# Attention and a mixture of experts in one kernel: the exponentials' transposes directly behind the scores, the other turns last

## The chip, the cores and the metric

The kernel runs on one core of one Trainium2 chip. A core has five engines with an instruction stream each: TensorE (PE, matrix products; its weight loads are listed as PEld), VectorE (DVE), ScalarE (ACT), GpSimd (POOL) and SyncE (SP, which only issues DMAs). Data lies in HBM, in SBUF, and, for results of TensorE, in PSUM banks. The metric is the device time of one execution in microseconds; times are given as the median of several runs.

## The reference

Attention over q, k, v of 4 x 8 heads, 576 rows and 64 columns, with a memory part, feeds a mixture of experts; the casts and the setup are left out:

```python
scores = scale * np.matmul(q, k.transpose(0, 1, 3, 2))
scores = np.where(causal, -1000000000.0, scores)
a = np.exp(scores - scores.max(-1, keepdims=True))
a /= a.sum(-1, keepdims=True) + 1e-09
local = np.matmul(a, v)
q_p = phi(q)                       # x + 1 for x > 0, else exp(x)
mem_ret = np.einsum('bhsd,bhde->bhse', q_p, M_prev)
mem_norm = np.einsum('bhsd,bhd->bhs', q_p, z_prev)[..., None] + 1e-06
x = g * (mem_ret / mem_norm) + (1 - g) * local     # g = sigmoid(beta), by head
...
noisy_logits = x @ w_gate + np.log1p(np.exp(x @ w_noise)) * noise
top2 = np.argpartition(-noisy_logits, 2, axis=1)[:, :2]
for e in range(8):
    for k in range(2):
        mask = top2[:, k] == e
        h = np.maximum(x[mask] @ w1[e], 0.0)
        out[mask] += top2_w[mask, k, None] * (h @ w2[e])
```

The x that goes into the experts has 2304 rows of 512 columns; each expert's hidden layer has 1024.

## The kernel before

Products are made in float32 out of three products of split operands: a high part (names ending in `h`), and the rest (`l`). So scores are `kT` times `qh`, `ql`, `qh` (L540; L531 for the short row blocks), and an expert's products are named `ha`, `hb` (first layer, L928) and `y` (second layer, L941).

**Attention.** A batch has 576 rows, five row blocks: four of 128 rows and a short one of 64. A row block's eight heads are cut into units: two units of four heads for the first two blocks, four units of two heads for the others. A unit's path is: scores on TensorE; row maxima with the mask on VectorE (L546); exponentials on ScalarE (L569, one instruction and a read of the row's sum per head); `trans`, which turns the exponentials by transposes on TensorE into a bank `tpa` (L587), four 128 x 128 blocks to a bank, and empties it on ScalarE into `aT` (L588); and the product with V into `avT` (L609).

The loop runs over units, as a pipeline: in one round, unit u + 1 has its exponentials, unit u its transposes, u - 2 its product with V, and u + 2 its scores. Beside this pipeline, each row block has work of its own that is done in the rounds. `q_turn` and `k_turn` transpose q and k (`tpq`, `tpk`, L420) and ScalarE reads them out (`qf`, L452, and `kf`, L427); of `kf` come the high and low halves `kT` (L432, L433; for the short block on ScalarE and VectorE, for the others on GpSimd). `tpm` (L477) is the memory part, read out by ScalarE as `mm` (L480). When all units of a block are done, ScalarE copies the output (`xo`, L618), `out_turn` transposes it (`tpo`, L642) and VectorE reads it out with the sums' reciprocals (`xr`, L644, L646). Then the block's logits follow in steps, held in a queue `xq`: x is transposed (`tpx`, L136), read out in two halves `xTlh` (ScalarE, L139) and `xTll` (VectorE, L140), multiplied with the gate's weights (`tpl`, L147 and L148), read out (`lt`, L150), transposed back (`tpL`, L155) and read out (`ll`, L157). At the end of a batch the routing starts: small VectorE steps, and products (`pp`, L227) of a mask `M` with a triangle to count slots. They stand in a queue `small`, from which a round takes two while a flag `fast` is set (for the third batch's routing). `puts` writes slots' row numbers into tables in HBM with GpSimd DMAs; gathers by GpSimd (L816) bring the rows of an expert, which `xprep` transposes (`tpm` of L865).

All turns (`tpa`, `tpo`, `tpq`, `tpk`, `tpm`, `tpx`, `tpl`, `tpL`, `pp`) share one pool of three PSUM banks. TensorE's order is that in which the code is written, since its instructions are chained; the other engines' orders are set by the scheduler. The weights of the first expert (`w0q` and `w0k`) are loaded and split (`w2ha`, `w2hb`, L892) during the last row blocks.

What else a round does beside scores and product with V was put into a list `xs`, in this order:

```python
xs = due                                    # out_turn of a finished block
# ... xprep, sums, fills, ev (q_turn, k_turn, memory, ...) by their due times
for _ in range(1 if c < len(chunks) - 2 else 2):
    if xq: xs.append(xq.popleft())          # a logit step
xs += trans(u)
if len(xq) > 3 and c < len(chunks) - 2:
    xs.append(xq.popleft())
```

**Experts.** Each expert has 608 slots in five tiles, three of 128 and two of 112. They run in passes (an expert and some of its tiles; the first four passes are (0; 0, 1, 2), (1; 0, 1, 2), (1; 3, 4), (0; 3, 4)), each in eight slots f, one per 128 of the hidden width. A tile's rows are turned in time for its pass: at its `begin` slot VectorE casts them and SP issues two DMA transposes (`trn`, L1028), at its `ready` slot ScalarE copies them (`xf`, L1039) and makes `xTh` (L1042), and VectorE makes `xTl` (L1043). A table names the slots (p, f) of both for passes 1 to 4.

Of the kernel before, what the change touches and what calls it, by code (L numbers as in the profile page):

```python
# [46 lines left out]
def tile_attention_moe(ctx: ExitStack, tc: tile.TileContext, q, k, v, M_prev, z_prev, beta,  # L47
# [78 lines left out]
    puts = deque()  # L126
    R = {"XT0": []}
# [190 lines left out]
    def attention():  # L318
        with ExitStack() as c2:
# [31 lines left out]
            chunks = [(b, i) for b in range(B) for i in range(NCH)]  # L351
# [344 lines left out]
            fills, small, xq, held = deque(), deque(), deque(), deque()  # L696
# [34 lines left out]
            def smalls():  # L731

                for _ in range(2 if R.get("fast") else 1):
                    if small:
                        in_turn(small.popleft())

# [7 lines left out]
            for u in range(NU + 2):  # L744
                if u + 1 < NU:
                    expo(u + 1)
                ys, end = [], []
                due = [held.popleft()] if held else []
                if u >= 2:
                    ys += av(u - 2)  # L750
                    cl = units[u - 2][0]
                    if u > NU or units[u - 1][0] != cl:
                        ys.append(lambda cl=cl: out_copy(cl))
                        (held if cl < len(chunks) - 3 else end).append(lambda cl=cl: out_turn(cl))
                if u + 2 < NU:
                    ys += score(u + 2)
                n_ = next((k_ for k_, f in enumerate(ys) if f.__name__ == "products"), len(ys) - 1) + 1
                ys = [lambda fs=ys[:n_]: [f() for f in fs]] + ys[n_:] + end
                xs = due
                if u >= NU - 2 and u <= NU:  # L760
                    xs.append(lambda t=u - NU + 2: xprep(R["XT0"], R["xgE"][t], t))
                if u < NU:
                    c, hs = units[u]
                    if u == first[c]:
                        on_chunk(c)
                    if chunks[c] == (B - 1, 4) and u == first[c]:
                        for f in range(2):
                            W0.append(load_w(None, 0, f, None, None, [
                                ap_.tile([P, H, D], F32, tag=nm + "n", name="w0" + nm, bufs=4) for nm in "kq"]))
                    if chunks[c] == (B - 1, 4) and u == first[c] + 1:  # L770
                        W0[:] = [split_w(ep, W0[0], "a", 1), split_w(ep, W0[1], "b", 1)]
                    if chunks[c][1] == 4 and (u + 1 == NU or units[u + 1][0] != c):
                        xs.append(lambda c=c: sums(c))
                    la = 4 if u < 3 else 7
                    nxt = units[u + la][0] if u + la < NU else -1
                    while any(f[0] <= nxt for f in fills):
                        xs.append(fills.popleft()[1])
                    while ev and ev[0][0] < TU[u + 1]:
                        xs.append(ev.popleft()[2])
                    for _ in range(1 if c < len(chunks) - 2 else 2):  # L780
                        if xq:
                            xs.append(xq.popleft())
                    if puts:
                        xs.append(lambda: puts and puts.popleft()())
                    xs += trans(u)
                    if len(xq) > 3 and c < len(chunks) - 2:
                        xs.append(xq.popleft())
                    if puts and R.get("fast"):
                        xs.append(lambda: puts and puts.popleft()())
                nx, ny = len(xs), max(1, len(ys))  # L790
                done = 0
                for y, f in enumerate(ys):
                    in_turn(f)
                    smalls()
                    while done * ny < (y + 1) * nx:
                        in_turn(xs[done])
                        done += 1
                        smalls()
                for f in xs[done:]:
                    in_turn(f)  # L800
# [95 lines left out]
    def experts(tail):  # L896
        with ExitStack() as c3:
# [152 lines left out]
                    gather_y(g, tall[:, e, t, 1:2], e * CAP)  # L1050

            begin, ready = {}, {}
            for p, l in ((1, ((0, (0, 1), (0, 4)), (1, (0, 2), (0, 5)), (2, (0, 3), (0, 6)))),
# [4 lines left out]
                for t, s_, e_ in l:  # L1058
                    begin.setdefault(s_, []).append((p, t))
                    ready.setdefault(e_, []).append((p, t))  # L1060
# [107 lines left out]
            with tc.For_i(0, over, 1):  # L1168
# [6 lines left out]
                with tc.For_i(1, nround, 1) as r:  # L1175
                    with tc.For_i(0, E, 1) as e:
# [26 lines left out]
                        for t in every:  # L1203
# [9 lines left out]
                                in_offset=None, bounds_check=NTOK - 1, oob_is_err=False)  # L1213

    tail = attention()
    experts(tail)


# [26 lines left out]
```

## Time and profile before

| | before |
|---|---|
| median of 3 runs | 743.59 us (743.22 to 746.72) |
| profiled execution: its time | 748.14 us |
| its span | 746.4 us |
| mean granted clock of TensorE | 0.974 |
| TensorE busy | 696.5 us (93%), 5046 instructions |
| weight loads busy | 598.2 us (80%) |
| VectorE busy | 453.1 us (61%) |
| ScalarE busy | 378.7 us (51%) |
| GpSimd busy | 366.8 us (49%) |

The span runs from the first instruction's start to the last one's end in the profiled execution; 1.7 us of its time lie outside. Attention fills the span to about 287 us, the experts the rest. The granted clock is the share of TensorE's full speed that the chip let it run at. A busy share is a mean over both parts and says little of either.

### The profile page before, as it was taken

What the parts mean: (1) busy time and instruction counts of PE and PEld (TensorE: products, weight loads), DVE (VectorE), ACT (ScalarE), POOL (GpSimd) and SP (SyncE); (2) the same over time, 40 slices, a digit from 0 to 9 for tenths busy, and PEclk for the clock granted to TensorE, in tenths of its full rate; (3) what the DMA queues carried; (4) which work ended last, traced back from release to release, by engine and by line L of the source; (5) the groups of instructions that cost most, each with busy time, mean ns of one, the idle gap of its engine ahead of it and who ended that gap; (6) DMA issues with size and microseconds to landing.
All of it is one profiled execution on the core that took longest, in us unless ns stands there. A gap on an engine that the chain in (4) does not pass through costs nothing. (4 is left out here: it accounts for less than half of the span.)

```text
span 746.4 us, 14446 instructions
## 1 busy us (share of the span) xinstructions
PE 696.5 (93%) x5046; PEld 598.2 (80%) x5046; DVE 453.1 (61%) x1232; ACT 378.7 (51%) x949; POOL 366.8 (49%) x378
## 2 busy tenths in 40 slices
PE   5999989998889789989999999999999999999993
PEld 4778767876777578879788888898889889988992
DVE  5675777568677667967694687454455355454312
ACT  4797778787768653445554144153253163162210
POOL 6424434641843544565354686843833734625502
PEclk8899999999989999999999999999999999999997
DMA  7634521251300045869995595693694694665201
GB/s 167 140 93 107 123 64 42 62 126 45 72 30 28 11 138 148 190 140 264 180 247 151 140 234 150 177 210 115 182 197 135 163 218 148 190 128 172 71 0 63
DMA packets 174287, 98.19 MB, mean 132 GB/s; under 512 B 113172, under 2 KB 152596, under 8 KB 174208
## 3 DMA queue, kind: packets, MB, share of 16 engines
q1 hardware_dynamic: 164128, 78.23, 42.6%
q0 software_dynamic: 10080, 18.98, 10.3%
q8 instruction: 42, 0.69, 0.4%
q14 instruction: 37, 0.30, 0.1%
HBM read 74.41 MB, written 22.54 MB: 130 GB/s over the span
## 5 line engine op out<-in xcount | busy, mean ns | idle before, releaser
L891 POOL TENSOR_TENSOR w1lm<-w1sm,w1hm 128x512 fp32r<-128x512 f32 x72 | 93.4, 1301 | 115.2 <-DVE w1hm L890 62.4
L941 PE MATMUL y<-w2hm,hTh 128*128 128x512 f32 (+1 forms) x310 | 122.2, 394 | 1.2 <-ACT hTh L931 1.2
L941 PE MATMUL y<-w2hm,hTl 128*128 128x512 f32 (+1 forms) x310 | 122.3, 394 | 0.4 <-DVE hTl L932 0.4
L941 PE MATMUL y<-w2lm,hTh 128*128 128x512 f32 (+1 forms) x310 | 121.5, 392 | 0.0
L546 DVE CUSTOM_DVE_ANT_0 sc<-sc,mask 128x128 f32<-128x128 f32 (+4 forms) x144 | 75.3, 524 | 48.9 <-PE sc L531 21.1
L931 ACT ACTIVATE hTh<-ha 128x304 fp32r<-128x304 f32 (+2 forms) x64 | 27.2, 426 | 147.0 <-PE ha L928 146.9
L892 ACT CAST w2hm<-w2sm 128x512 fp32r<-128x512 f32 x74 | 45.8, 619 | 97.8 <-PE y L941 97.8
L893 DVE TENSOR_TENSOR w2lm<-w2sm,w2hm 128x512 fp32r<-128x512 f32 x74 | 61.5, 831 | 52.0 <-ACT w2hm L892 52.0
L569 ACT ACTIVATE a<-sc,nb 128x128 f32<-128x128 f32 (+4 forms) x144 | 79.1, 566 | 11.2 <-DVE nb L546 5.8
L890 DVE CAST w1hm<-w1sm 128x512 fp32r<-128x512 f32 x74 | 37.0, 499 | 62.5 <-PE hb L928 45.7
L587 PE MATMUL tpa<-identr,a 128*128 128x128 f32 x400 | 61.3, 287 | 13.8 <-DVE xr L644 4.7
L928 PE MATMUL ha<-xTl,w1hm 128*128 128x304 f32 (+2 forms) x224 | 68.9, 307 | 2.0 <-DVE xTl L1043 2.0
L941 PEld LDWEIGHTS y<-w2hm,hTl 128*128 128x128 f32 (+1 forms) x310 | 56.5, 182 | 17.1 <-DVE hTl L932 2.1
L928 PE MATMUL ha<-xTh,w1hm 128*128 128x304 f32 (+2 forms) x224 | 68.5, 306 | 1.0 <-DVE hTl L932 0.6
L928 PE MATMUL hb<-xTh,w1hm 128*128 128x304 f32 (+2 forms) x224 | 68.7, 307 | 0.0
L928 PE MATMUL ha<-xTh,w1lm 128*128 128x304 f32 (+2 forms) x224 | 68.2, 304 | 0.0
L928 PE MATMUL hb<-xTl,w1hm 128*128 128x304 f32 (+2 forms) x224 | 67.9, 303 | 0.0
L928 PE MATMUL hb<-xTh,w1lm 128*128 128x304 f32 (+2 forms) x224 | 67.7, 302 | 0.0
L941 PEld LDWEIGHTS y<-w2hm,hTh 128*128 128x128 f32 (+1 forms) x310 | 56.6, 183 | 12.3 <-ACT hTh L931 1.3
L941 PEld LDWEIGHTS y<-w2lm,hTh 128*128 128x128 f32 (+1 forms) x310 | 56.6, 183 | 11.5
L588 ACT COPY aT<-tpa 128x512 f32<-128x512 f32 x120 | 57.4, 527 | 14.6 <-PE tpa L587 13.7
L609 PE MATMUL avT<-aT,vt 128*64 128x128 f32 (+1 forms) x960 | 60.7, 270 | 1.3 <-ACT xo L618 1.3
(240 smaller groups left out, 1631.7 us busy)
## 6 DMA issues: line engine op xcount, KB each, us to landing
w1sm<-in_moe_w_dram SPq DMA_DIRECT2D x74, 256.0 KB, 3.2
w2sm<-in_moe_w_dram SPq DMA_DIRECT2D x74, 256.0 KB, 4.0
y_scratch<-o SPq DMA_DIRECT2D x21, 256.0 KB, 3.8
vt<-in_v_dram SPq DMA_DIRECT2D x16, 256.0 KB, 4.6
xall_scratch<-xr SPq DMA_DIRECT2D x16, 256.0 KB, 2.2
kn<-in_k_dram SPq DMA_DIRECT2D x15, 256.0 KB, 2.9
qn<-in_q_dram SPq DMA_DIRECT2D x15, 256.0 KB, 3.4
y_scratch<-o SPq DMA_DIRECT2D x14, 224.0 KB, 4.9
```

The lines of the kernel that those rows point to most:

```text
L546: nc.vector.tensor_tensor_reduce(out=s_, in0=s_, in1=mask4 if i == 4 else mask[:, 512 - W:512], scale=-1.0, scalar=3.0e38, op0=ALU.add, op ...
L569: nc.scalar.activation(o_.rearrange("p (t n) -> p t n", t=2) if d["i"] == 4 else o_, s_, AF.Exp, scale=-1.0, bias=st["nb"][:, x_:x_ + 1], ...
L587: nc.tensor.transpose(tp[:, x_ * P:(x_ + 1) * P], a[:, (g + x_) * P:(g + x_ + 1) * P], ident)
L588: nc.scalar.copy(aT[:, g:g + w, :].rearrange("p b t -> p (b t)"), tp[:, 0:w * P])
L609: nc.tensor.matmul(o_[k_ * 64:(k_ + 1) * 64, h0 // 2, 0:n], CH[c0 + j]["v"][:, h0 + k_, :], r_, start=(j == 0), stop=(j == i))
L890: nc.vector.tensor_copy(h1, a)
L891: R["w1l"] = lo.tensor_tensor(out=l1, in0=a, in1=h1.bitcast(F32), op=ALU.subtract)
L892: nc.scalar.copy(h2, b_)
L893: nc.vector.tensor_tensor(out=l2, in0=b_, in1=h2.bitcast(F32), op=ALU.subtract)
L928: nc.tensor.matmul(o, w_[:, c, :], xT[xi][:, c, c0_ - at:c1_ - at], start=(c == 0 and i_ == 0), stop=(c == 3 and i_ == 2))
L931: R["hh"] = nc.scalar.activation(hT[0][:, c0_:c1_], o, AF.Relu)
L941: nc.tensor.matmul(ys[t][0:b_ - a_], hT[hi][:, a_:b_], w_, start=(f == 0 and i_ == 0), stop=(f == FF // P - 1 and i_ == 2))
```

## The change

Three places are edited. First, in a round of attention one logit step and `trans` are put at the head of the list, directly behind the unit's product with V and scores, as `lead`; the output's turn, the turns of q and k, the memory part and the rest follow; and a second logit step, when the queue holds more than two (more than one in the last two row blocks), stands last, as `rear`. Second, while `fast` is set and the next small routing step has a TensorE product, the queue `small` stands still until it has been asked eight times (once). Third, the table of the experts' turns: pass 1 a slot sooner, passes 2 to 4 later at their ends.

```diff
             def smalls():
                 for _ in range(2 if R.get("fast") else 1):
+                    if small and getattr(small[0], "pe", False) and R.get("fast"):
+                        R["wait"] = R.get("wait", 0) + 1
+                        if R["wait"] < 8:
+                            return
                     if small:
                         in_turn(small.popleft())
...
-                xs = due
+                xs, lead, rear = due, [], []
...
+                    if xq:
+                        lead.append(xq.popleft())
+                    lead += trans(u)
...
-                    for _ in range(1 if c < len(chunks) - 2 else 2):
-                        if xq:
-                            xs.append(xq.popleft())
-                    if puts:
-                        xs.append(lambda: puts and puts.popleft()())
-                    xs += trans(u)
-                    if len(xq) > 3 and c < len(chunks) - 2:
-                        xs.append(xq.popleft())
-                    if puts and R.get("fast"):
-                        xs.append(lambda: puts and puts.popleft()())
+                    for _ in range(2 if R.get("fast") else 1):
+                        if puts:
+                            xs.append(lambda: puts and puts.popleft()())
+                    if len(xq) > 1 if c >= len(chunks) - 2 else len(xq) > 2:
+                        rear.append(xq.popleft())
+                xs = lead + xs + rear
...
-            for p, l in ((1, ((0, (0, 1), (0, 4)), (1, (0, 2), (0, 5)), (2, (0, 3), (0, 6)))),
-                         (2, ((3, (1, 0), (1, 3)), (4, (1, 1), (1, 4)))),
...
+            for p, l in ((1, ((0, (0, 0), (0, 3)), (1, (0, 1), (0, 4)), (2, (0, 2), (0, 5)))),
+                         (2, ((3, (1, 1), (1, 4)), (4, (1, 2), (1, 6)))),
...
```

In the rows below a line number of the changed kernel is 3 or 4 higher from L735 on.

TensorE, in a round of the second batch in which the short row block's keys are turned. Before, behind the scores (`sc`):

```order
L540 MATMUL sc<-kT,qh 128x512 x2
L540 MATMUL sc<-kT,ql 128x512 x2
L540 MATMUL sc<-kT,qh 128x512 x2
L420 MATMUL tpk<-identr,kn 128x64 x4
L147 MATMUL tpl<-xTlh,wgs 32x128
L148 MATMUL tpl<-xTll,wgs 16x128
...
L587 MATMUL tpa<-identr,a 128x128 x8
```

And of the change:

```order
L540 MATMUL sc<-kT,qh 128x512 x2
L540 MATMUL sc<-kT,ql 128x512 x2
L540 MATMUL sc<-kT,qh 128x512 x2
L155 MATMUL tpL<-identr,lt 128x32
L587 MATMUL tpa<-identr,a 128x128 x8
L420 MATMUL tpk<-identr,kn 128x64 x4
L609 MATMUL avT<-aT,vt_122 64x128 x2
```

The eight transposes `tpa` now come ahead of `tpk`, directly behind the scores and one short logit step; the products of the logits have moved to another round.

ScalarE, at the same keys. Before:

```order
L618 COPY xo<-avT 128x512
L427 ACTIVATE kf<-tpk 128x4x64
L432 CAST kT<-kf 128x4x64
L150 COPY lt<-tpl 32x128
L588 COPY aT<-tpa 128x512 x2
```

And of the change:

```order
L588 COPY aT<-tpa 128x512 x2
L427 ACTIVATE kf<-tpk 128x4x64
L569 ACTIVATE a,den<-sc,nb 128x512
L432 CAST kT<-kf 128x4x64
L569 ACTIVATE a,den<-sc,nb 128x512
```

The two read-outs of `tpa` now come ahead of the keys' read-out `kf`, and an exponential stands between `kf` and the cast into `kT`.

TensorE again, in the round of the third batch's routing product `pp`. Before:

```order
L540 MATMUL sc<-kT,qh 128x512 x2
L420 MATMUL tpq<-identr,qn 128x64 x4
L477 MATMUL tpm<-mz,qpT 128x130 x2
L227 LDWEIGHTS tri
L227 MATMUL pp<-M,tri 128x40
```

And of the change:

```order
L540 MATMUL sc<-kT,qh 128x512 x2
L155 MATMUL tpL<-identr,lt 128x32
L587 MATMUL tpa<-identr,a 128x128 x6
L227 LDWEIGHTS tri
L227 MATMUL pp<-M,tri 128x40
...
L420 MATMUL tpq<-identr,qn 128x64 x4
L477 MATMUL tpm<-mz,qpT 128x130 x2
```

`pp` stays in its round; the last logit step and the transposes are ahead of it now, and the turns of q and the memory part behind it.

ScalarE, in the experts where a pass ends. Before, the end of pass 0 with the last turn for pass 1 (tiles of 128), and the first `hTh` of pass 1:

```order
L931 ACTIVATE hTh<-hb 128x384
L1039 COPY xf<-trn 128x512 x2
L1042 CAST xTh<-xf 128x4x128
L892 CAST w2hm<-w2sm 128x512
L931 ACTIVATE hTh<-ha 128x384
```

And of the change, the end of pass 1 with the last turn for pass 2 (a tile of 112), and the first `hTh` of pass 2:

```order
L934 ACTIVATE hTh<-hb 128x384
L1042 COPY xf<-trn 128x512 x2
L1045 CAST xTh<-xf 128x4x112
L934 ACTIVATE hTh<-ha 128x224
```

The last turn for pass 2 now has the place ahead of its pass that the last turn for pass 1 had before; that of pass 1 is a slot further from its own.

## Rows read from the trace of the kernel before

**Rows 1.** Busy time by engine in four stretches (from:to, length, PE, PEld, ...).
```profile
core 0: us, PE busy (x) PEld busy (x) DVE busy (x) ACT busy (x) POOL busy (x), PEclk, DMA share, GB/s
...
18.00:200.00 182.00, 168.78 (x1717) 137.95 (x1716) 126.80 (x477) 144.70 (x424) 81.22 (x87) 0.98 0.37 87
200.00:287.00 87.00, 74.32 (x759) 60.35 (x758) 57.33 (x231) 55.99 (x169) 38.31 (x43) 0.92 0.18 55
...
320.00:400.00 80.00, 76.00 (x434) 66.79 (x434) 55.61 (x87) 41.27 (x77) 41.32 (x34) 0.98 0.90 206
400.00:736.00 336.00, 334.44 (x1906) 297.42 (x1904) 171.99 (x302) 113.03 (x222) 173.74 (x170) 1.00 0.60 153
```
**Rows 2.** Groups of TensorE instructions, 18 to 287 us: busy, mean, idle before.
```profile
L587 PE MATMUL tpa<-identr,a 128*128 128x128 f32 x400 | 61.3, 287 | 13.8 <-DVE xr L644 4.7 <-ACT mm L480 3.0 <-ACT aT L588 1.8
L609 PE MATMUL avT<-aT,vt 128*64 128x128 f32 (+1 forms) x960 | 60.7, 270 | 1.3 <-ACT xo L618 1.3
...
L147 PE MATMUL tpl<-xTlh,wgs 128*32 128x128 f32 (+1 forms) x76 | 12.1, 236 | 2.0 <-ACT xTlh L139 2.0
L136 PE MATMUL tpx<-identr,xr 128*128 128x128 f32 (+1 forms) x76 | 11.7, 278 | 0.5 <-DVE ww L183 0.5
L148 PE MATMUL tpl<-xTll,wgs 128*16 128x128 f32 (+1 forms) x76 | 10.8, 222 | 1.6 <-DVE xTll L140 1.2 <-DVE ar L638 0.5
...
L155 PE MATMUL tpL<-identr,lt 32*128 32x32 f32 (+1 forms) x19 | 4.6, 242 | 1.6 <-ACT lt L150 1.6
...
L227 PE MATMUL pp<-M,tri 128*128 128x40 bf16 (+1 forms) x4 | 0.7, 183 | 2.6 <-DVE M L209 2.6
```
**Rows 3.** Timeline of TensorE, a wait for a bank (start, duration, [idle <-releaser]).
```profile
208.44 0.76 PE L587 MATMUL tpa<-identr,a 128*128 128x128 f32 x5 [1.81 <-DVE xr L644]
```
**Rows 4.** Timeline of TensorE, a pair of logit products.
```profile
252.48 0.25 PE L147 MATMUL tpl<-xTlh,wgs 128*32 128x128 f32 x1 [0.67 <-ACT xTlh L139]
253.41 0.23 PE L148 MATMUL tpl<-xTll,wgs 128*16 128x128 f32 x1 [0.68 <-DVE xTll L140]
```
**Rows 5.** Timeline of TensorE, the third batch's routing product.
```profile
246.35 0.18 PE L227 MATMUL pp<-M,tri 128*128 128x40 bf16 x1 [2.63 <-DVE M L209]
```
**Rows 6.** Busy time in four short stretches; the granted clock stands behind POOL.
```profile
208.40:216.40 8.00, 7.96 (x76) 7.12 (x78) 4.99 (x21) 5.20 (x22) 3.61 (x4) 0.58 0.21 69
246.30:250.90 4.60, 4.55 (x39) 3.54 (x38) 3.65 (x24) 2.71 (x9) 0.77 (x2) 0.63 0.01 2
277.00:281.80 4.80, 4.23 (x38) 3.48 (x38) 0.95 (x3) 1.05 (x4) 0.00 (x0) 0.64 0.76 242
322.80:326.00 3.20, 3.13 (x10) 3.13 (x11) 0.62 (x2) 0.00 (x0) 0.00 (x0) 0.54 0.78 120
```
**Rows 7.** Timeline of ScalarE and TensorE, the first expert's weights.
```profile
202.11 0.62 ACT L892 CAST w2hb<-w0q 128x512 fp32r<-128x512 f32 x1 [2.01 <-DMA w0q<-in_moe_w_dram]
...
203.28 0.33 PE L587 MATMUL tpa<-identr,a 128*128 128x128 f32 x1 [1.63 <-ACT ll L157]
```
**Rows 8.** Timeline of all engines, the short row block's keys in the second batch.
```profile
117.79 0.69 ACT L569 ACTIVATE a<-sc,nb 128x512 f32<-128x512 f32 x1
...
118.13 0.40 PE L420 MATMUL tpk<-identr,kn 64*128 64x64 f32 x4
...
118.68 0.69 DVE L546 CUSTOM_DVE_ANT_0 sc<-sc,mask 128x512 f32<-128x512 f32 x1
...
120.08 0.42 DVE L433 TENSOR_TENSOR kT<-kf,kT 128x256 fp32r<-128x256 f32 x1
...
120.99 0.54 PE L531 MATMUL sc<-kT,q4h 128*128 128x288 f32 x2
```
**Rows 9.** Timeline of POOL and TensorE, the first expert's rows.
```profile
269.36 1.00 POOL L816 DMA_INDIRECT xw<-xall_scratch,tabE  x1 [0.30 <-issue]
...
274.62 0.66 PE L865 MATMUL tpm<-identr,xw 128*128 128x128 f32 x4
```
**Rows 10.** Waits of TensorE, 287 to 746 us (total, times, longest).
```profile
PE ha L928 <- DVE xTl L1043: 2.0, 1, 2.0
PE y L941 <- ACT hTh L931: 1.2, 1, 1.2
```

6 rows, old and new, of the table g are left out of this document.

## The prediction

> **What bounds the kernel now.** I read the table of stretches first. From 400 to 736 us, in the experts, TensorE is busy 334.4 of 336 us at full clock, and the change edits nothing there; from 18 to 200 us it is busy 168.8 of 182, from 200 to 287 us 74.3 of 87, and from 320 to 400 us 76 of 80 [rows 1]. So the kernel is bound by TensorE, and an edit that keeps its work can only win idle time or clock: 13.2 + 12.7 = 25.9 us of idle time in attention and 4.0 us where the experts' first passes end. Against ScalarE there is less room than that: it is busy 144.7 us of the first 182, so TensorE's 168.8 is only 24 us above it.
>
> The second view is TensorE's groups of instructions between 18 and 287 us, with the idle time before each. Of the 25.9 us, 13.8 stand before the exponentials' transposes (L587), 2.0 + 0.5 + 1.6 + 1.6 = 5.7 before the steps of the logits (L147, L136, L148, L155), and 2.6 before the one routing product `pp` (L227) [rows 2]. The remaining 3.8 wait for `xo` and for keys.
>
> Third, the timeline at such places, to see what is late. At 208.44 the exponentials have long been there, yet `tpa` stands idle for 1.81 us, released by VectorE's `xr` (L644) [rows 3]: that is the instruction that empties the bank of `tpo`. All turns share three banks, the unit before puts `tpo`, `tpq` and `tpm` right ahead of `tpa`, and so `tpa`, the fourth, waits until the first is read out. For the logits, the product with the hi half waits 0.67 us for `xTlh`, the one behind it 0.68 us for `xTll` [rows 4]: both are made from `tpx`, which ran directly ahead. `pp` waits 2.63 us for the mask `M` [rows 5].
>
> [...]
>
> **The change, part by part.** No instruction is added or removed; the terms are idle time and clock.
>
> (a) *Exponentials' transposes directly behind the scores.* Of the 13.8 us, 1.63 + 1.81 = 3.4 belong to (d). For the other 10.4, `tpa` now has the unit's attention-times-V product and scores between itself and the last turn, so the banks are empty. The other turns come last, and wait in turn for ScalarE to empty `tpa`'s banks. Bounds: nothing remains (-10.4), or the read-out of these banks, one per unit and more, takes back 7 (-3.4). I take -7.5: a unit's last turn finds the banks of `tpa` read out unless ScalarE is behind. With the output's turn its store of x, too, is issued later on SP by one `tpa`, some 0.9 us; only the gather of (f) reads it, much later.
>
> (b) *Logit steps.* One step leads a unit and another may end it, so the pair of [rows 4] comes apart by a unit, and the 5.7 us go, but `tpx` as leading step now needs `xr` of the unit just before, which comes late in it. Bounds -5.7 and 0; I take -3, with 2.7 for the new waits of `tpx` and `tpL` (16 row blocks at under 0.2 each).
>
> (c) *`pp`.* The order shows it in the same unit, behind the six transposes, while the logits and the routing that precede `M` start a unit sooner. Its 2.63 us are covered, and with them the slow stretch behind it: -2.6 - 1.7 = -4.3. The far bound is 0: if VectorE makes `M` later by as much, nothing is won. I take -4.3, since the six transposes alone are 6 x 61.3/400 = 0.9 us and a unit more is some 4.
>
> (d) *The weights of the first expert.* At 202.11 ScalarE waits 2.01 us for a DMA (`w0q`), holds `ll` up, and TensorE loses 1.63 us at 203.28 [rows 7], then 1.81 [rows 3], then clock [rows 6]. The same split steps stand in the same unit, and their load is queued on SP in the same place; the wait stays. 0, with bounds -2 and +2: moving `tpa` ahead of `tpq` shifts by one transposition what waits.
>
> (e) *Keys of the short row block.* This is the edit that costs. Before, `tpk` (118.13) stands right behind the scores, and `kT`, four steps later, ends at 120.08 + 0.42 = 120.50, 0.49 us before the scores at 120.99 that need it [rows 8]. Now eight transposes stand ahead of `tpk`, and an exponential of 0.69 us between `kf` and the cast on ScalarE. Only the 16 products with V (16 x 60.7/960, about 1.0 us [rows 2]) and `tpk` itself (0.40) lie between `tpk`'s start and the scores, while the chain took 2.37 us, and with the exponential 2.37 + 0.69 = 3.1. Bounds per batch: 3.1 - 1.4 = 1.7, or 0 if in the 2.37 us both engines were at other work that now comes earlier. I take 1.1, four times: +4.4.
>
> (f) *Gather of the first expert's rows.* Behind `pp` come VectorE's row numbers, ten writes of POOL's queue, a load on SP and three gathers on POOL, the last issued at 269.36; the first `tpm` that turns the rows stands at 274.62, 5.3 us later, without a wait [rows 9]. The gathers' transfer lies in these 5.3 us, the rest is slack. TensorE has lost waits of (b) and (a) on the way there, some 3 to 4 us, the POOL chain has not. Bounds 0 and +2.5; I take +1.
>
> (g) *Clock.* The 277 us stretch follows logit waits as in (b); it may be half undone: -0.8 (0 to -1.7).
>
> (h) *Expert turns.* TensorE waits 2.0 us for `xTl` and 1.2 for `hTh` there [rows 10], with a slow stretch of 1.5 behind the first [rows 6]. The last turn of pass 1 moves a slot ahead, which cures the first wait; but the last turn of pass 2 now stands where that of pass 1 stood, right ahead of the pass's first use (ScalarE's order above). So a like wait can reappear. The turns' DMA transposes are issued on SP ahead of two weight loads while the DMA engines are 0.90 busy [rows 1]; loads come a few us later and are held in advance, so I price them at 0, with +2 if not. Bounds -4.7 and +2; I take -2.
>
> Sum: -7.5 - 3 - 4.3 + 4.4 + 1 - 0.8 - 2 = -12.2. ScalarE's share rises as TensorE's idle time goes: 144.7 in 182 - 9 = 173 is 84%, and in the units where both have about equal work there is no slack. I take off 2.5: -9.7. The profiled execution took 748.14 us (span 746.4 and 1.7 around it), so it would take 738.4. It is itself 4.6 us above the median of the runs shown, 743.59; with the same gain that is 733.9, about **734 us**.
>
> One more cost is possible, since more transposes now stand in one row. There are 400 of L587 alone, 61.3 us of work [rows 2], and the stretch that holds most of them had a granted clock of 0.98 [rows 1], so they are priced at nothing. [...]
>
> **The rivals.**
> 1. *The wait only moves* (0.14). TensorE is let go sooner but ScalarE, 24 us short of it, sets the pace: a = -3.4, b = 0, c = -4.3, e = +4.4, f = +2.5, g and h = 0: -0.8, or 743 us. For it: ScalarE's 144.7 of 182; against it: most of its own waits are for TensorE's turns, which come sooner.
> 2. *The clock falls* (0.04). Now `tpa`, `tpo`, `tpq` and `tpk` stand in one row. If the first stretch were granted 0.92 like the second [rows 1], its work would cost 168.8 x (0.98/0.92 - 1) = 11 us more: 734 + 11 = 745 us. Against it: `tpo`, `tpq` and `tpa` stood in a row before, at 0.98. [...]
> 3. *Slower: the short row block's keys* (0.12). If VectorE also has two score maxima (0.69 us each) in front of `kT` [rows 8], each of four waits is 1.1 + 1.4 = 2.5 us, about as long as that before `pp`, and is followed by half clock like it: 1.7 to 3.4 us each. Then (e) is 4 x 4.2 to 4 x 5.9 = 17 to 24 instead of 4.4: 734 + 12 to 734 + 19, 746 to 753 us. The gain is gone when a batch's keys cost (9.7 + 4.4)/4 = 3.5 us.
> 4. *In the experts the change doesn't do what it says* (within the forecast): pass 2 takes over pass 1's wait, and (h) is 0: 736 us.
> 5. *All terms at their good end* (0.12): a -10.4, b -5.7, e +2, f 0, h -4.7: 734 - 2.9 - 2.7 - 2.4 - 1 - 2.7 = 722 us.
>
> **How the numbers follow.** The forecast has 0.58; its own range, 726 to 740 us, lets the terms (a) to (h) miss by some 7 together. Half a per cent, 739.9 to 747.3, is what a measurement of this kernel can tell from no change. Faster holds the forecast and rival 5: 0.70. Same: rivals 1 and 2 and the lower edge of 3, 0.19. Slower: 0.11. For eight in ten the range goes from rival 5 to the near end of rival 3: 722 to 747.
>
> **What would show it.** Right: before L587 between 18 and 287 us idle falls from 13.8 to under 6; no wait before `pp` and clock 1.0 behind it; the waits for `xTlh` and `xTll` gone; a new wait of about 1 us before the scores of L531 at each batch's end; the same wait for `ll` near 200 us; experts from 400 us on unchanged. Wrong would be: idle before L642, L420 and L477 as great as what L587 lost (then rival 1), waits of over 2 us for `kT` (rival 3), or a lower clock with no waits ahead of it (rival 2).

## The result, and the profile after

The change makes the kernel slower. Fifteen executions of each on one chip gave a median of 751.46 us (747.67 to 754.9) against 746.72 for the kernel before; the ratio is 1.0065 with a 95% interval from 1.0041 to 1.0089. The forecast was 734 us (722 to 747), faster. The profiled execution of the changed kernel has a span of 752.3 us, 5.9 more than before.

The two kernels' stages don't stand at the same times, so I compare from the same work to the same work: from the second unit of the second row block's scores to the last scores of all. The table of stretches has for the kernel before

```profile
23.23:271.90 248.67, 225.59 (x2304) 183.25 (x2304) 171.80 (x654) 191.24 (x569) 114.62 (x123) 0.97 0.29 71
```

and for the changed kernel, from the same view,

```profile
23.93:279.38 255.45, 228.33 (x2305) 183.15 (x2304) 180.29 (x652) 191.14 (x569) 108.01 (x118) 0.97 0.26 65
```

The same TensorE instructions took 6.8 us longer: TensorE stood still for 27.1 us (255.45 - 228.33) where it did for 23.1, and its busy time is 2.7 us longer. What lies behind this stretch is 1.6 us shorter (752.3 - 279.4 = 472.9 against 746.4 - 271.9 = 474.5). So the loss is in attention.

TensorE's groups between 18 and 287 us, which answer to [rows 2], show where the idle time went (busy, mean ns, then idle before). Four groups of the kernel before that [rows 2] leaves out:

```profile
L477 PE MATMUL tpm<-mz,qpT 128*128 128x130 f32 (+1 forms) x160 | 27.0, 307 | 0.0
...
L642 PE MATMUL tpo<-identr,xo 128*128 128x128 f32 (+1 forms) x80 | 12.8, 282 | 0.6 <-ACT xo L618 0.5
...
L420 PE MATMUL tpq<-identr,qn 128*128 128x128 f32 (+1 forms) x72 | 10.4, 266 | 0.0
L420 PE MATMUL tpk<-identr,kn 128*128 128x128 f32 (+1 forms) x72 | 10.0, 261 | 0.0
```

And the changed kernel:

```profile
L609 PE MATMUL avT<-aT,vt 128*64 128x128 f32 (+1 forms) x920 | 58.7, 270 | 2.7 <-ACT xo L618 2.7
L587 PE MATMUL tpa<-identr,a 128*128 128x128 f32 x395 | 57.0, 283 | 0.0
...
L477 PE MATMUL tpm<-mz,qpT 128*128 128x130 f32 (+1 forms) x160 | 27.2, 309 | 5.0 <-ACT aT L588 2.7 <-DVE xTll L140 1.2 <-ACT kf L427 0.8
...
L642 PE MATMUL tpo<-identr,xo 128*128 128x128 f32 (+1 forms) x76 | 12.6, 291 | 3.1 <-ACT lt L150 3.0
L147 PE MATMUL tpl<-xTlh,wgs 128*32 128x128 f32 (+1 forms) x76 | 11.9, 226 | 0.3 <-ACT aT L588 0.3
L420 PE MATMUL tpq<-identr,qn 128*128 128x128 f32 (+1 forms) x72 | 11.7, 288 | 4.4 <-ACT aT L588 4.2
L136 PE MATMUL tpx<-identr,xr 128*128 128x128 f32 (+1 forms) x76 | 11.1, 268 | 1.1 <-DVE M L207 1.0
L420 PE MATMUL tpk<-identr,kn 128*128 128x128 f32 (+1 forms) x72 | 10.9, 273 | 2.5 <-DVE lg L158 1.5 <-ACT lt L150 0.7
L148 PE MATMUL tpl<-xTll,wgs 128*16 128x128 f32 (+1 forms) x76 | 10.6, 220 | 5.6 <-DVE xTll L140 5.6
```

The exponentials' transposes (L587) wait no more: 13.8 us became 0.0. But the four groups of turns that now stand behind them wait 5.0 + 3.1 + 4.4 + 2.5 = 15.0 us, where they had 0.6 before. The releaser is mostly ScalarE, which reads out the transposes' own banks (`aT`, 2.7 + 4.2 us) or the logits (`lt`, 3.0 + 0.7). This window holds less of the changed kernel's work (920 products with V against 960). The same view over the two stretches with the same work gives, for L587 and the four groups together, 13.2 us before and 15.0 after.

Two places repeat in several batches. In the timeline of the changed kernel (all engines; start, duration) they look like this, with the short row block's keys in the last two rows:

```profile
92.33 1.09 PE L587 MATMUL tpa<-identr,a 128*128 128x128 f32 x8
...
92.78 0.47 ACT L569 ACTIVATE a<-sc,nb 128x256 f32<-128x256 f32 x1 [0.98 <-DVE mr L486]
...
93.25 0.60 PE L642 MATMUL tpo<-identr,xo 128*64 128x128 f32 x4
...
94.15 0.48 ACT L569 ACTIVATE a<-sc,nb 128x256 f32<-128x256 f32 x1
...
94.60 1.09 ACT L588 COPY aT<-tpa 128x512 f32<-128x512 f32 x2
...
95.25 0.66 PE L420 MATMUL tpq<-identr,qn 128*128 128x128 f32 x4 [1.39 <-ACT aT L588]
...
111.90 0.21 ACT L183 ACTIVATE ex<-ex 128x5 f32<-128x5 f32 x1 [2.50 <-DVE ex L183]
112.01 0.24 ACT L150 COPY lt<-tpl 32x128 f32<-32x128 f32 x1
...
112.31 0.66 PE L642 MATMUL tpo<-identr,xo 128*128 128x128 f32 x4 [1.52 <-ACT lt L150]
...
126.79 0.42 ACT L432 CAST kT<-kf 128x256 fp32r<-128x256 f32 x1
...
127.26 0.40 PE L531 MATMUL sc<-kT,q4h 128*128 128x288 f32 x1 [0.22 <-ACT kT L432]
```

At 92.33 the transposes fill two banks, `tpo` the third; `tpq` is the fourth turn and needs the first bank. ScalarE has stood still for 0.98 us for VectorE, is then at four exponentials until 94.6 and reads the banks only after them, and `tpq` loses 1.39 us. At 111.90 ScalarE stood still for 2.50 us: the next instruction in its queue was a small exponential of the routing, for which VectorE had not made the input, and the read-out `lt`, whose data was there (the last `tpl` ended at 110.13 us), stood behind it and began at 112.01.

The clock, for the places of [rows 6] that moved (granted clock behind the five engines):

```profile
179.50:183.50 4.00, 3.68 (x22) 3.12 (x24) 2.56 (x13) 2.74 (x9) 0.61 (x1) 0.57 0.05 19
244.00:260.00 16.00, 14.73 (x145) 11.10 (x143) 14.20 (x65) 12.09 (x36) 3.11 (x4) 1.00 0.10 34
260.00:340.00 80.00, 74.92 (x566) 65.01 (x563) 60.15 (x200) 41.67 (x98) 45.32 (x45) 1.00 0.55 149
```

The slow stretches behind `pp`, near 277 us and near 322 us are gone, and there is a new one right behind the third batch's wait of `tpo` for `lt`. The four `tpo` that open it (clock 0.50 from 180 to 183 us) took 1.07 us at 179.82, where those of 112.31, at a clock of 1.00, took 0.66. If all work there is slower by the share of the clock that is missing, the stretch costs 4.0 x 0.43 = 1.7 us, an estimate.

### The profile page after: what moved, and what is told of

It reads as the page before. It is cut to its first block, busy times and chain, and to the rows that moved or that the text cites. A ratio compares the mean times of both kernels' runs of the same rounds, so it can differ in the third digit from the quotient of the medians.

```text
span 752.3 us, 14441 instructions
## 1 busy us (share of the span) xinstructions
PE 697.9 (93%) x5046; PEld 597.3 (79%) x5046; DVE 463.5 (62%) x1232; ACT 379.3 (50%) x949; POOL 363.3 (48%) x378
## 5 line engine op out<-in xcount | busy, mean ns | idle before, releaser
L896 DVE TENSOR_TENSOR w2lm<-w2sm,w2hm 128x512 fp32r<-128x512 f32 x74 | 66.5, 899 | 55.5 <-ACT w2hm L895 55.5
L1028 DVE COPY pl<-xg 128x512 uint16<-128x512 uint16 x74 | 45.6, 660 | 26.9 <-DMA trn<-pl 26.4
```

The lines of the kernel that those rows point to most:

```text
L896: nc.vector.tensor_tensor(out=l2, in0=b_, in1=h2.bitcast(F32), op=ALU.subtract)
L1028: nc.vector.tensor_copy(pl[:, h_], xv[:, h_])
```

## The experiments

Ratios are to the kernel before, run in turn with each on the same chip, with 95% intervals. The first eight runs were on chips on which the kernel before took 769.5 and 771.6 us; all traces there have a few waits of 2 to 9 us in attention, at the short row blocks, that neither trace above has. What they are no run tells. They are in these eight ratios, and they differ from kernel to kernel: the three longest are 7.6, 6.1 and 5.7 us with the transposes alone, and 4.9, 3.4 and 2.6 in the change, on the same chip. So the size of a single ratio of these eight is less sure than its interval says; which of the two moves loses is also borne out by the last four runs, whose traces have no such waits.

**The table of expert turns alone.** The kernel before with the new table of the change, all else as it was.

```diff
-            for p, l in ((1, ((0, (0, 1), (0, 4)), (1, (0, 2), (0, 5)), (2, (0, 3), (0, 6)))),
+            for p, l in ((1, ((0, (0, 0), (0, 3)), (1, (0, 1), (0, 4)), (2, (0, 2), (0, 5)))),
...
```

> The kernel before with the new table of expert turns and nothing else. Theory: the table is a small gain or nothing and the loss lies in attention, so attention up to 287 us is as before and the experts are 0 to 3 us shorter: ratio 0.996 to 1.000. Rival, that the table costs something that the whole change's attention hides: ratio above 1.003.

Measured: 1.0021 (0.9991 to 1.0052). Neither a gain nor a loss that can be told: the interval reaches into the ranges of both.

**The transposes first, the logit steps in their old places** (with the change's other edits).

```diff
-                    if xq:
-                        lead.append(xq.popleft())
                     lead += trans(u)
...
+                    for _ in range(1 if c < len(chunks) - 2 else 2):
+                        if xq:
+                            xs.append(xq.popleft())
+                    if len(xq) > 3 and c < len(chunks) - 2:
+                        rear.append(xq.popleft())
```

> The change with the exponentials' transposes directly behind the scores, but the logit steps where they were (one in the middle, a second one last when more than three are queued). Theory that the wait for a bank only moves to the fourth turn of a unit: idle before L587 near 0, and 10 us or more before L642, L420 and L477 together, so attention alone is not shorter; ratio 0.998 to 1.006. Rival, that the logit steps' new places are what costs (7 us of waits for xTll and lt): those waits go and the kernel gains 5 us or more, ratio under 0.996.

Measured: 1.0086 (1.0059 to 1.0112). Slower than either said. The rival's gain did not come, so the logit steps' new places are not what costs.

**The logit steps first and last, the transposes in their old place** (with the change's other edits).

```diff
                     if xq:
                         lead.append(xq.popleft())
-                    lead += trans(u)
...
+                    xs += trans(u)
                     if len(xq) > 1 if c >= len(chunks) - 2 else len(xq) > 2:
                         rear.append(xq.popleft())
```

> The change with the logit steps at the head and the end of a unit, but the exponentials' transposes behind the other turns as before. Theory: the waits for xTll of some 5 us stand as in the change, since a step that ends a unit and one that leads the next are only a product with V and scores apart; the waits of L587 are back at 10 us or more, and ratio is 1.002 to 1.008. Rival, that the logit steps cost nothing: waits for xTll under 2 us and ratio 0.996 to 1.001.

Measured: 0.9963 (0.9937 to 0.9989): faster. My theory failed, and the rival holds. In this trace the waits for `xTll` were 0.8 us for the logits and 0.5 for `tpa`, not 5.6.

**The next unit's exponentials written behind the transposes.**

```diff
-                if u + 1 < NU:
-                    expo(u + 1)
...
+                if u + 1 < NU:
+                    lead.append(lambda u=u: expo(u + 1))
                 xs = lead + xs + rear
```

> The change with the next unit's exponentials written behind the transposes, so that on ScalarE the two read-outs of tpa come after three of four exponentials (of the second row block) where they came after four, and similar moves by one place elsewhere. Theory that the moved waits come from ScalarE's order (read-outs behind exponentials): the three waits of 1.39 us of tpq for aT shrink by about one exponential, 0.45 us each, and the whole by 1 to 3 us against the change: ratio 1.000 to 1.006. Rival, that the read-outs would be as late without the exponentials ahead: these waits stay at 1.39 us.

Measured: 1.0087 (1.0056 to 1.0119). One of the three `tpq` waits fell to 0.76 us, the other two stayed at 1.42, and the time is no better than the change's. A move by one exponential settles nothing.

**Each move by itself, on the kernel before**, the transposes alone:

```diff
-                    xs += trans(u)
...
+                if u < NU:
+                    xs = trans(u) + xs
```

> The kernel before with one move alone: the exponentials' transposes directly behind the scores. Theory that this move is the loss: before L587 TensorE waits under 3 us where it waited 13.8, the waits show up before L477, L420 and L642 instead, and the ratio is 1.004 to 1.010. Rival, that the move gains in itself and the loss comes from its meeting with the new places of the logit steps: ratio 0.990 to 1.000.

and the logit steps alone:

```diff
-                    for _ in range(1 if c < len(chunks) - 2 else 2):
-                        if xq:
-                            xs.append(xq.popleft())
+                    if xq:
+                        lead.append(xq.popleft())
...
-                    if len(xq) > 3 and c < len(chunks) - 2:
-                        xs.append(xq.popleft())
+                    if len(xq) > 1 if c >= len(chunks) - 2 else len(xq) > 2:
+                        rear.append(xq.popleft())
+                xs = lead + xs + rear
```

> The kernel before with one logit step at a unit's head and a second one at its end, and nothing else. Theory: the steps come a unit earlier and the pp product's wait of 2.6 us and its half-speed stretch go; ratio 0.992 to 0.998. Rival, that the gain of the run with the transposes in their old place came from the expert turns and not from the logit steps: ratio 0.999 to 1.003.

Measured: the transposes alone 1.0093 (1.0057 to 1.0129), the logit steps alone 0.9960 (0.9932 to 0.9988). Both ratios lie in the theories' ranges. Added, they give 0.93 - 0.40 = 0.53%; the whole change on the same chip gave 0.58%. Since each of the two is known to some 0.3%, and the whole has the routing's edit and the table besides, the close agreement is luck; it only says that the sum is not contradicted. One part of the second expectation failed: `pp` still waited 2.2 us. TensorE's waits with the transposes alone, 18 to 310 us, have these rows:

```profile
PE tpL L155 <- ACT lt L150: 6.1, 3, 2.5
...
PE tpq L420 <- ACT aT L588: 3.6, 3, 1.2
PE pp L227 <- DVE M L209: 2.8, 1, 2.8
PE tpk L420 <- DVE xTll L140: 2.1, 3, 1.2
...
PE tpa L587 <- DVE xr L644: 0.5, 1, 0.5
```

`tpa` is free there, too, and a step of the logits that had the transposes ahead of it (`tpL`) now follows close behind `tpl` and waits for `lt`. The waits before L477, L642 and L420 came as well, but the longest of them are among those that only these chips have.

**Two read-outs from ScalarE to VectorE**, in the change:

```diff
-                    nc.scalar.copy(aT[:, g:g + w, :].rearrange("p b t -> p (b t)"), tp[:, 0:w * P])
+                    (nc.vector.tensor_copy if i == 1 and g == 0 else nc.scalar.copy)(
+                        aT[:, g:g + w, :].rearrange("p b t -> p (b t)"), tp[:, 0:w * P])
...
-            nc.scalar.copy(lt[:, 0:n], tp[0:4 * E, 0:n])
+            nc.vector.tensor_copy(lt[:, 0:n], tp[0:4 * E, 0:n])
```

> The change with two kinds of read-outs taken from ScalarE to VectorE: the first bank of the exponentials' transposes in the second row blocks (aT), and the logits' lt. Theory that the fourth turn of a unit waits because ScalarE reads the banks only behind its exponentials: the three waits of tpq for aT (1.39 us each) and the two of tpo for lt (1.52 us each) go or fall under 0.7 us, and 2 to 6 us of the loss come back: ratio to the kernel before 0.999 to 1.005. Rival, that any engine is as late there because its maxima stand ahead too: these waits stay over 1 us, now for VectorE, ratio 1.006 to 1.010.

Measured: 1.0155 (1.0117 to 1.0193), much slower, and slower than either said. Its waits, 18 to 310 us:

```profile
PE tpk L420 <- DVE lt L150: 7.6, 5, 2.0
PE tpl L148 <- DVE xTll L140: 5.6, 7, 1.1
PE tpo L643 <- DVE lt L150: 5.5, 4, 1.6
```

For `lt` the rival holds: VectorE was later with it (7.6 + 5.5 us of waits) than ScalarE was in the change (0.7 + 3.0). The waits of 1.39 us of `tpq` for `aT` went, as the theory has it (what the view still lists of this kind is 3.6 + 0.3 us), but no time came back.

**The change again**, beside the three before.

> The changed kernel as it is, beside the three others on one chip. Theory: 1.005 to 1.009 as in the first measurement, and all of it in attention. Rival, that the loss belongs to the chip of the first measurement: 0.995 to 1.001.

Measured: 1.0058 (1.0031 to 1.0085). The loss is not a matter of one chip.

The last four runs were on a chip on which the kernel before took 745.5 us, without those extra waits.

**The transposes alone, with the read-out of their first bank on VectorE** in the second row blocks:

```diff
-                    xs += trans(u)
...
+                    xs = trans(u) + xs
...
-                    nc.scalar.copy(aT[:, g:g + w, :].rearrange("p b t -> p (b t)"), tp[:, 0:w * P])
+                    (nc.vector.tensor_copy if i == 1 and g == 0 else nc.scalar.copy)(
+                        aT[:, g:g + w, :].rearrange("p b t -> p (b t)"), tp[:, 0:w * P])
```

> The kernel before with the exponentials' transposes directly behind the scores, and one read-out taken from ScalarE to VectorE: the first bank of these transposes in the second row blocks. Theory that the first bank stays full because its read-out stands behind exponentials on ScalarE: the three waits of tpq for aT, 3.9 us in the run with the move alone, fall under 1 us; ratio 1.003 to 1.009. Rival, that they are as late on VectorE: 3 us or more of waits of tpq remain, ratio over 1.009.

Measured: 1.0070 (1.0044 to 1.0096). The waits of `tpq` for `aT` are gone from the list (18 to 280 us):

```profile
PE tpL L155 <- ACT lt L150: 6.1, 3, 2.5
...
PE tpm L477 <- DVE aT L588: 1.1, 3, 0.4
...
```

So ScalarE's late read-out is the cause of that wait: of 3.6 us in the run with the move alone, 1.1 are left, before `tpm`, for the same read-out on VectorE. Removing it doesn't make the move a gain. The rest of the loss can be read here, from the same work to the same work, and from two of the stretches behind the waits of 2.5 us of `tpL` for `lt`:

```profile
24.18:277.86 253.68, 228.80 (x2304) 185.36 (x2304) 186.77 (x660) 187.56 (x561) 112.36 (x125) 0.96 0.28 69
116.00:120.00 4.00, 4.00 (x36) 3.23 (x34) 2.86 (x14) 2.21 (x5) 0.00 (x0) 0.66 0.02 6
184.00:188.00 4.00, 4.00 (x34) 3.39 (x35) 3.33 (x15) 2.87 (x7) 0.00 (x0) 0.63 0.01 4
```

It takes 5.0 us more than in the kernel before, of which 1.8 are idle time. Most of the rest goes with the clock, whose mean is 0.96 for 0.97: an estimate from the two means is 253.68 x 0.04 - 248.67 x 0.03 = 2.7 us. In the kernel before the clock is 1.00 from 116 to 120 and from 184 to 188 us, so with the slow work behind them, 4.0 x 0.34 = 1.4 and 4.0 x 0.37 = 1.5 us by the same kind of estimate, the waits cost more than their own length.

**The output's turn ahead of the transposes**, in the change:

```diff
                 due = [held.popleft()] if held else []
+                held_due = list(due)
...
-                xs = lead + xs + rear
+                xs = xs[:len(held_due)] + lead + xs[len(held_due):] + rear
```

> The change with the output's turn ahead of the leading logit step and the exponentials' transposes, everything else as in the change. Theory that a unit's fourth turn waits for the first bank, and that this wait is short where VectorE reads the first bank (tpo): the waits of tpq for aT (4.2 us) and of tpo for lt (3.0 us) go, those of tpm remain; ratio 0.998 to 1.004. Rival, that the waits are a matter of how much is to be read out in a unit and not of what stands first: the sum of waits is as in the change (30 to 35 us without those over 2 us), ratio 1.004 to 1.009.

Measured: 1.0108 (1.0081 to 1.0136). The theory failed. `tpq` hardly waits for `aT` now (0.2 us), and `tpo` not for `lt`, but (18 to 280 us)

```profile
PE tpm L477 <- ACT aT L588: 7.2, 9, 1.5
PE tpl L148 <- DVE xTll L140: 5.9, 7, 1.1
PE tpa L587 <- DVE xr L644: 4.1, 7, 1.0
PE tpq L420 <- DVE xr L644: 3.7, 6, 2.7
```

The rival is nearer, though its own numbers missed too: TensorE stood still for 28.4 us in the stretch with the same work, where it did for 27.1 in the change, and the ratio lies above the rival's range. In these two orders, which turn stands first decides who waits, and hardly how much.

**The first expert's weights split where they are written**, on the kernel before. An order is added on ScalarE and VectorE (`R["aT"]` and `R["top"]` are the last read-out of the transposes and the last maximum).

```diff
-                        W0[:] = [split_w(ep, W0[0], "a", 1), split_w(ep, W0[1], "b", 1)]
+                        with tc.issue_after(R["aT"].ins), tc.issue_after(R["top"].ins):
+                            W0[:] = [split_w(ep, W0[0], "a", 1), split_w(ep, W0[1], "b", 1)]
```

> The kernel before with the first expert's weights split at the end of attention, where they are written, in place of 60 us earlier. Theory that the load of w0q holds up ScalarE there and TensorE loses 1.6 + 1.8 us and then some 3 us at half speed: all three go, 5 to 7 us less, ratio 0.990 to 0.995. Rival, that the waits only go to the next turn or that the split work hurts as much at its new place: ratio 0.997 to 1.003.

Measured: 0.9983 (0.9961 to 1.0005). The stall near 203 us and its slow stretch are gone (stretches, and a row of the waits):

```profile
200.00:212.00 12.00, 10.67 (x134) 8.88 (x130) 8.48 (x34) 7.62 (x26) 8.93 (x11) 1.00 0.26 74
268.00:284.00 16.00, 11.22 (x109) 8.66 (x106) 10.00 (x32) 7.69 (x21) 6.18 (x7) 0.79 0.40 125
```
```profile
PE tpx L136 <- DVE r L183: 2.6, 1, 2.6
```

Near 275 us `tpx` waits 2.6 us for VectorE, where it waited 0.5 before, and the clock of the stretch from 268 to 284 us is 0.79; in the kernel before it was 0.89 there. The waits went as the theory has it, but the time lies in the rival's range. Whether the weights' new place makes VectorE late near 275 us, no run tells.

**Logit steps first and last, the routing's edit and the late split together**, on the kernel before; the transposes stay last and the old table of expert turns stays.

```diff
+                    if small and getattr(small[0], "pe", False) and R.get("fast"):
+                        R["wait"] = R.get("wait", 0) + 1
+                        if R["wait"] < 8:
+                            return
...
+                        with tc.issue_after(R["aT"].ins), tc.issue_after(R["top"].ins):
...
+                        lead.append(xq.popleft())
...
+                xs = lead + xs + rear
```

> The kernel before with the logit steps at a unit's head and end, the routing's later products as in the change, and the first expert's weights split late; the exponentials' transposes stay last. Theory: the gains add up, 0.4% of the logit steps and 0.5 to 0.9% of the weights: ratio 0.986 to 0.993. Rival, that one stall takes the place of the other: ratio 0.994 to 0.998.

Measured: 0.9946 (0.9924 to 0.9968), 742.07 against 745.5 us: faster than the kernel before and, by the ratios, than the change, but within the rival's range: the gains didn't all add up. From the same work to the same work as above:

```profile
24.32:265.00 240.68, 220.86 (x2305) 178.48 (x2304) 171.47 (x654) 192.61 (x567) 107.19 (x115) 0.99 0.28 70
200.00:216.00 16.00, 14.24 (x182) 12.34 (x181) 11.88 (x45) 11.70 (x40) 9.08 (x10) 1.00 0.20 59
```

That is 8.0 us less than the kernel before in this stretch, of it 3.3 of idle time; the clock is 0.99 instead of 0.97 (1.00 where the weights' stall was), and `pp` no longer waits. Some of it is given back later. `tpa` still waits there, more than before (15.6 us in this stretch against 13.1):

```profile
PE tpa L587 <- DVE xr L644: 6.7, 9, 1.2
PE tpa L587 <- ACT mm L480: 4.9, 6, 1.1
PE tpa L587 <- ACT lt L150: 2.9, 3, 1.2
```

## Why the prediction was wrong, step by step

- **(a), the step that failed.** It is "a unit's last turn finds the banks of `tpa` read out unless ScalarE is behind", with at most 7 us taken back. ScalarE was behind, though not for want of time (it is busy 191.1 of the 255.5 us): it read the banks only after its exponentials, or after a routing step that waited for VectorE. The idle time of L587 and of the four turns together was 14.4 us (13.8 + 0.6) before and 15.0 after between 18 and 287 us, and 13.2 and 15.0 in the same work, with what belongs to (d) in it. So the -7.5 was +1.8. The bound of -3.4 was no bound: I let the read-outs take back 7 us and they took back all. The sign that the prediction named for it came: idle before L642, L420 and L477 grew by 14.4 us, and L587 lost 13.8. Rival 1, "the wait only moves", had the mechanism and the wrong price: its sum was a gain of 0.8 us.
- **(b).** -3 was forecast. The idle time of the four logit groups went from 5.7 to 0.3 + 5.6 + 1.1 + 0.0 = 7.0 us, and from 4.2 to 6.0 in the same work: +1.8. The steps did come apart, but with the transposes moved a step that ends a unit and the one that leads the next have only a product with V and scores between them, and `xTll` stands on VectorE behind maxima (two of 0.55 and 0.57 us, and routing steps, ahead of that of 176.32, for which `tpl` waits 0.55 us). With the transposes last the same move of the logit steps gains 0.4%, and the waits of the logits for `xTll` are 0.8 us: by their waits the two moves can't be priced one by one.
- **(c).** Right: `pp` waits 0.7 us, and the clock behind it is 1.00; -1.9 - 1.7 = -3.6 for -4.3. The single runs show that the routing's edit has a part in it, since with the logit steps alone 2.2 us of wait stayed; with both and the transposes last, none did.
- **(d).** Right: the wait stayed. ScalarE waited 1.63 us for `w0q` at 212.22, and TensorE 0.7 + 1.5 us before `tpk`; the slow stretch stayed too (clock 0.50 from 216 to 220 us).
- **(e).** The mechanism was right and the size off: 0.22 us, three times, 0.7 in place of 4.4. The last two rows of the timeline show why: the wait is for the cast on ScalarE, which began 0.94 us after `kf` did (125.85), and VectorE had nothing ahead of its part. The cast ended 1.98 us after `tpk` began (125.23), and the products with V and a first score product, which began at 126.64 without a wait, covered all but 0.22 us of that. Behind the three waits (59.74, 127.26 and 196.28 us) the clock stayed at 1.00. Rival 3, the slower case, is out with it: that the measured 751 us falls into its range of 746 to 753 is chance.
- **(f).** No wait for the gathers; `tpm` of the expert's rows waited 0.6 us, for `aT`. Forecast +1.
- **(g).** Better than forecast at its place, where the slow stretch went wholly (by the estimate 1.7 us for 0.8), but the new stretch at 180 us took the 1.7 us back.
- **(h).** -2 was forecast; the table alone is 1.0021, within its interval nothing. In the change, what lies behind the attention stretch is 1.6 us shorter, with (g) in it: its busy time fell by 3.2 us, as the slow stretches near 277 and 322 us went, and its idle time grew by 1.6. The waits changed owner, as rival 4 had it (292 to 752 us):

```profile
PE ha L931 <- DVE hTl L935: 2.2, 1, 2.2
PE ha L931 <- DVE dl L238: 1.5, 1, 1.5
PE ha L931 <- DVE xTl L1046: 1.3, 1, 1.3
PE y L944 <- DVE hTl L935: 1.1, 2, 0.7
```

- **The clock's price.** The 1.7 us in (c) and in the bound of (g), the 1.5 us in (h) and the 1.7 to 3.4 us in rival 3 are my estimate from [rows 6], length times the missing share of the clock: 4.6 x 0.37, 4.8 x 0.36, 3.2 x 0.46 and, for 3.4, 8.0 x 0.42. No run shows these terms by themselves. What the traces show is the clock: before, 0.50 from 247.5 to 250.5 us, behind `pp`; in the change 1.00 from 244 to 340 us, so behind `pp` and near 277 and 322 us, and 0.57 from 179.5 to 183.5 us.
- **Rival 2**, the clock, did not come: 0.97 in both. That more transposes in one row could lower the clock was my assumption, and no run shows it. What precedes each fall of the clock in attention, from 24 us on, in these two traces is a wait of TensorE, or several, the longest of them 0.7 to 2.6 us (1.81 us at 208.44 and 2.63 at 246.35 before, 1.52 at 179.82 and 1.54 at 213.17 in the change). No run has a long stretch of transposes alone that would test it.

Of the attention stretch's 6.8 us, 4.0 are idle time. By groups, with rounding, it is +1.8 in the turns, +1.8 in the logits, -1.9 before `pp`, +0.7 for the keys, and two things that no term priced: +1.4 of products with V that wait for `xo` (1.3 to 2.7 us) and +0.3 of scores.

What stays open is the other part. The busy time grew by 2.7 us, and not by the clock, whose mean is 0.97 in both. Nor did the instructions get longer: count times mean, added up over TensorE's groups of this stretch, is 660 us in both kernels. So they overlap less, and no run tells at which changes from one kind of instruction to the next. And what keeps VectorE and ScalarE late whatever the order, I only argue from the orders that were tried: the idle time of this stretch was 19.8 to 28.4 us in the six kernels measured without those extra waits.

## What to carry to other kernels

Here a wait for a shared bank that ended when another engine had read it out was that engine's lateness (3.6 us of it became 1.1 with the read-out on VectorE); with three banks, a new order on the waiting engine handed the wait to the turns that now stand behind (L587 went from 13.8 us to 0.0, the four turns from 0.6 to 15.0). Before pricing such a move as a gain, look in the reader's queue for what stands ahead of the read-out (exponentials, a small step that waits for a third engine). And try each part alone: here one part of an edit gained 0.4% and the other lost 0.7 to 0.9%.

## What the runs showed of the hardware that was not expected

- A 5-column exponential held ScalarE up for 2.50 us, with read-outs behind it whose data was there.
- The kernel before took 745.5 us on one chip and 771.6 on another. The change was traced on two chips: 752.3 and 774.0 us. From the same work to the same work its idle time is 27.1 and 45.6 us, 13.0 us of the second in four waits of 2 to 5 us that the first doesn't have, and its busy time 228.3 and 234.4, at a clock of 0.97 and 0.95. The ratios agreed across the chips (1.0065 and 1.0058 for the change).
- The same stall of 1.52 us of `tpo` was followed by 4 us at a clock of 0.57 near 180 us, and by no such stretch near 112 us (clock 1.00 from 112 to 116 us); where the stall near 203 us was taken away, the clock stayed at 1.00 from 200 to 212 us.
